# First half batch of attention: output sums ahead of the second weight's joined words on VectorE, and the table for Sin loaded behind the last exponentials

## The chip, the cores and the metric

The kernel runs on one core of a Trainium2 chip (trn2). The metric is the device time of one launch in microseconds (us). The engines are TensorE (PE, with its weight loads as PEld), VectorE (DVE), ScalarE (ACT), GpSimd (POOL) and SyncE (SP, which issues most DMAs).

## The reference, cut to what matters

Three stages follow each other. `sm_attn` is a softmax over the scores times the values; the attention's output is the sum of a pooled and a local one. `w_in` and `w_out` are float64 arrays, the other inputs are float32.

```
# 4 batches, 8 heads, 576 positions, 64 features
out = repeat(sm_attn(q, k, v, each the mean of 4 positions), 4) + sm_attn(q, k, v, |i - j| < 4 only)
x   = out of all heads side by side             # 2304 tokens x 512
h   = x @ w_in                                  # 512 -> 2048
x   = (h * cos(h)) @ w_out                      # 2048 -> 512
e   = argmax(x @ w_gate)                        # one of 8 experts for each token
out = softmax(x @ w_gate)[e] * (relu(x @ w1[e]) @ w2[e])   # 512 -> 1024 -> 512
```

## The kernel before

The middle layer goes over 9 blocks of 256 tokens (i) and 8 pieces of the weights (fp). `hidden(i, fp)` takes 24 matmuls for h, in two float32r parts of x (`xh`, the rounded part, and `xl`, what is left) and two of the weight. Then it forms h·cos(h): ACT rounds h to whole turns (L401), DVE subtracts them (L402), ACT takes Sin (L403) and Square (L404), DVE multiplies (L405), ACT casts to `gh` (L408) and DVE makes the rest `gl` (L409). `project(i, fp)` adds 12 matmuls into the two accumulators of the block (`acc`, L423).

The weights arrive as the 64-bit words of float64. `convert_w(fp, which)` makes two float32r parts of each of the 16 pieces on DVE and POOL, in halves of 512 columns: shift and mask of the high word (L355), the low word's bits or-ed in (L357), the sign joined (L359: the *joined* words), a cast on POOL (L364) and the rest by subtraction on DVE (L366). In the rows of the scheduler's order, `w0_0`, `w1_0`, `w2_0` are pieces 0, 1 and 2 of `w_in` (called in-weights 0, 1, 2 below), and `w0_1`, `w1_1`, `w2_1` those of `w_out` (out-weights 0, 1, 2). Their words stand in `w32_0_1` (in-weight 1), `w32_1_0` (out-weight 0) and so on, with the kind ahead of the piece. The first six are converted in the order of `ORDER`: in 0, in 1, out 0, in 2, out 1, out 2.

The layer can begin when the first 256 tokens of x are there, which is the first half of batch 0 of the attention. So that half batch runs first, its 4 pairs of heads in turn by `together` (a count n goes up with each step of one of them): transposed queries (`tq`), scores (`s`, `sd`), exponentials (`p`, `pd`), their transposes (`pt`, `ptd`, copied by ACT to `pT`, `pdT`), outputs (`o`, L250 and L261), the output sum `xo` on DVE (L263) and then `first_x`, which makes `xh` on ACT (L322) and `xl` on DVE (L323). The first three weights are converted at n = 12, 20 and 28. The second half batch runs beside the first pieces of block 0; `hidden(1, 0)`, the fourth call of `hidden`, needs its x, and the load of the weights from piece 3 on is issued when it is through.

Every engine works off its own queue in order. The order in a queue is fixed when the program is built, by a scheduler; `issue_after(x)` tells it to set an instruction behind x. A wait of one instruction thus holds up all that stands behind it on its engine.

Of the kernel before, what the change touches and what calls it, by code (L numbers as in the profile page):

```python
# [8 lines left out]
F32 = mybir.dt.float32  # L9
# [4 lines left out]
AF = mybir.ActivationFunctionType  # L14
# [5 lines left out]
P = 128  # L20
# [3 lines left out]
NEARLY = 3  # L24
CONV = (12, 20, 28)
POOLED = (12, 12, 13, 14, 15, 16, 17, 18)
# [6 lines left out]
class Kernel:  # L33
# [134 lines left out]

    def queries(self, pool, n, n_, j, qs, raw, hp, kd, kT, vd, vw, sink, behind=None):

# [46 lines left out]
        for t in range(nd):  # L217
            nc.scalar.activation(pd[:m, t, :], ps[:m, t, :], AF.Exp, bias=mxd[:m, t:t + 1], accum_out=smd[:m, t:t + 1])
        self.scaled = nc.gpsimd.tensor_scalar(out=smd[:m, :nd], in0=smd[:m, :nd], scalar1=1e-9, scalar2=4.0,
# [38 lines left out]
        for i in range(nt):  # L258
            for par in range(2):
                r = slice(64 * par, 64 * par + 64)  # L260
                nc.tensor.matmul(ps[r, 64 * i:64 * i + 64], lhsT=vw(i, par), rhs=pT[:, i, r], start=True, stop=True)  # L261
        with self.tc.issue_after(behind()) if behind else nullcontext():
            nc.vector.tensor_tensor(  # L263
                out=x[:, :4 * ng].rearrange("p (g f) -> p g f", f=4),
                in0=ps[:, :4 * ng].rearrange("p (g f) -> p g f", f=4),
                in1=od[:, :ng].unsqueeze(2).to_broadcast([P, ng, 4]), op=ALU.add)
        sink(x)
# [78 lines left out]

    def convert_w(self, fp, which, behind=None):

        nc = self.nc
        t = self.stage.tile([P, 1040], I32, tag="w32", bufs=self.W32, name=f"w32_{which}_{fp}")  # L350
        two = self.words.pop((fp, which)).rearrange("p (n two) -> p n two", two=2)
        halves = [slice(512 * n, 512 * n + 512) for n in range(2)]
        for sl in halves:
            low, high = two[:, sl, 0], two[:, sl, 1]
            nc.vector.tensor_scalar(out=t[:, sl], in0=high, scalar1=3, scalar2=0x3FFFFFFF,  # L355
                                    op0=ALU.logical_shift_left, op1=ALU.bitwise_and)
            nc.vector.scalar_tensor_tensor(out=t[:, sl], in0=low, scalar=29, in1=t[:, sl],  # L357
                                           op0=ALU.logical_shift_right, op1=ALU.bitwise_or)
            self.joined = nc.vector.scalar_tensor_tensor(out=t[:, sl], in0=high, scalar=-0x40000000, in1=t[:, sl],  # L359
                                                         op0=ALU.bitwise_and, op1=ALU.bitwise_or).ins  # L360
        tile = self.w[fp, which] = self.tile_w(fp, which)
# [399 lines left out]
    def run(self):  # L761
# [99 lines left out]
        def first(hp, j):  # L861
            if j == 0:
                q, at = raw["q", 0], hp
            else:
                q, at = ap.tile([P, 4, P], F32, tag="raw", bufs=self.RAWS, name=f"rawq_{hp}"), None
                self.load_rows(q, self.q, 0, hp, 4 * self.HALF[1][0], self.QROWS[1])
            yield from self.queries(pp, 4, f"0_{hp}", j, lanes[hp], q, at, *kv[hp],
                                    lambda kj, par: vd[kj][:, 2 * hp + par, :], lambda i, par: vw[:, i, 2 * hp + par, :],
                                    lambda x: self.first_x(x, hp, j),
                                    (lambda: self.joined) if j == 0 else None)  # L870

        n = 0
        sums = self.summed_values(pp, psh, [raw["v", j] for j in range(2)])
        for _ in self.together([first(hp, 0) for hp in range(4)], 4):
            n += 1
            for _ in range(POOLED.count(n)):
                vd = next(sums)
            if n in CONV:
                with tc.issue_after(self.step):
                    self.convert_w(*early.pop(0), self.scaled)  # L880
        wide.close()
# [206 lines left out]
```

## Time and profile before

| | before |
|---|---|
| median of 3 runs | 876.47 us (875.76 to 877.15) |
| profiled execution | 877.69 us, of which 875.9 us are the span |
| mean granted TensorE clock | 0.979 |
| PE busy | 830.3 us (95%) |
| DVE busy | 537.7 us (61%) |
| ACT busy | 495.4 us (57%) |

The span reaches from the first to the last instruction of the profiled execution. Busy shares are means over the whole span; the first 100 us, where the change lies, are filled otherwise. Times below are us from the span's start.

### The profile page before, as it was taken

To read this page: it belongs to the slowest core of one execution; us is meant where nothing else is said; L and a number is where in the kernel's file an instruction comes from. 1 tells how busy PE (TensorE), PEld (TensorE's weight loads), DVE (VectorE), ACT (ScalarE), POOL (GpSimd) and SP (SyncE) were. 2 spreads that over 40 slices of the span, in tenths; PEclk is the share of its full clock that TensorE was granted. 3 is DMA by queue.
4 is the path that set the end of the run, shared out by engine and by line. 5 is a ranking of instruction groups with operands and counts; after the bars stand their busy time and mean duration, and the time that the engine had idled before them with its cause. 6 is when DMAs were issued, how large, how long until landed. Compare 5 with 4: busy or idle time off the path is not lost.

```text
span 875.9 us, 16801 instructions
## 1 busy us (share of the span) xinstructions
PE 830.3 (95%) x6130; PEld 711.9 (81%) x6130; DVE 537.7 (61%) x1293; ACT 495.4 (57%) x1246; POOL 197.6 (23%) x356
## 2 busy tenths in 40 slices
PE   6889799999999999999999999999899999999995
PEld 4667578778788888788898888898788888888895
DVE  5885799876444485476666657586447654555320
ACT  5466766676766875675644444583366544544321
POOL 5252344442222212313101010100121112012200
PEclk9989899999999999999999999999899999999998
DMA  9931783233252024022010101241748746446110
GB/s 202 290 79 38 295 247 96 71 82 85 59 167 64 14 76 105 13 73 73 15 49 1 49 1 49 73 123 47 192 143 292 243 135 212 148 160 198 58 38 22
DMA packets 112695, 95.87 MB, mean 109 GB/s; under 512 B 65120, under 2 KB 92844, under 8 KB 112604
## 3 DMA queue, kind: packets, MB, share of 16 engines
q1 hardware_dynamic: 108492, 83.96, 32.8%
q0 software_dynamic: 4112, 10.76, 4.1%
q8 instruction: 50, 0.82, 0.4%
q14 instruction: 41, 0.34, 0.1%
HBM read 81.31 MB, written 13.98 MB: 109 GB/s over the span
## 4 chain that ended last, share of the span: by engine, by line
PE 59%; DMA 6%; issue 5%; ACT 5%; DVE 5%; POOL 2%; POOLq 0%; DVEq 0%; ACTq 0%
PE acc L423 16%; PE h L395 15%; PE eacc L671 10%; PE eph L652 9%; DMA lists<-tokens,posi 2%; ACT p L203 1%; DMA raw<-in_moe_w_dram 1%; DMA out_dram<-y,ids 1%; PE o L261 1%; DVE prod L471 1%; PE o L250 1%; PE ext L631 1%; DMA rows<-rows,esrc 1%; PE ptd L238 1%; PE eph_late L689 1%
## 5 line engine op out<-in xcount | busy, mean ns | idle before, releaser
L395 PE MATMUL h<-xh,w 128*128 128x256 f32 x1152 | 230.0, 289 | 0.6 <-ACT xh L322 0.5
L423 PE MATMUL acc<-w,gh 128*128 128x512 f32 x576 | 191.5, 408 | 10.9 <-issue 4.5
L395 PEld LDWEIGHTS h<-xh,w 128*128 128x128 f32 x1152 | 185.8, 192 | 5.5 <-DVE w L366 0.9
L395 PE MATMUL h<-xl,w 128*128 128x256 f32 x576 | 165.4, 287 | 1.4 <-DVE xl L323 1.4
L423 PEld LDWEIGHTS acc<-w,gh 128*128 128x128 f32 x576 | 103.4, 190 | 30.6 <-issue 4.7
L423 PE MATMUL acc<-w,gl 128*128 128x512 f32 x288 | 117.6, 408 | 1.8 <-DVE gl L409 1.8
L652 PE MATMUL eph<-exh,w 128*128 128x256 f32 (+5 forms) x512 | 118.1, 307 | 0.0
L395 PEld LDWEIGHTS h<-xl,w 128*128 128x128 f32 x576 | 110.5, 192 | 4.2 <-DVE xl L323 1.6
L580 DVE TENSOR_TENSOR w<-raw,w 128x512 fp32r<-128x512 f32 x128 | 83.3, 687 | 32.5 <-ACT w L579 32.2
L671 PE MATMUL eacc<-w,hh 128*128 128x512 f32 (+4 forms) x304 | 99.2, 407 | 0.3 <-ACT hh L660 0.3
L652 PEld LDWEIGHTS eph<-exh,w 128*128 128x128 f32 x512 | 87.9, 190 | 3.3
L579 ACT CAST w<-raw 128x512 fp32r<-128x512 f32 x128 | 73.6, 618 | 29.3 <-DMA raw<-in_moe_w_dram 16.3
L401 ACT ACTIVATE u<-h 128x512 int32<-128x512 f32 x72 | 43.2, 600 | 79.7 <-PE h L395 79.6
L652 PE MATMUL eph<-exl,w 128*128 128x256 f32 (+5 forms) x256 | 78.7, 307 | 0.0
L405 DVE SCALAR_TENSOR_TENSOR u<-u,h 128x512 f32<-128x512 f32 x72 | 49.3, 684 | 47.6 <-ACT u L404 47.2
L402 DVE SCALAR_TENSOR_TENSOR u<-h,u 128x512 f32<-128x512 f32 x72 | 49.4, 686 | 38.5 <-ACT u L401 36.3
L471 DVE SCALAR_TENSOR_TENSOR prod<-row,wgb 128x512 f32<-128x512 f32 x96 | 67.1, 699 | 7.4 <-ACT row L465 6.0
L423 PEld LDWEIGHTS acc<-w,gl 128*128 128x128 f32 x288 | 54.5, 189 | 14.4 <-DVE gl L409 2.5
L408 ACT CAST gh<-u 128x512 fp32r<-128x512 f32 x72 | 44.6, 619 | 35.8 <-DVE u L405 21.3
L499 POOL DMA_INDIRECT lists<-tokens,posi x18 | 19.0, 1057 | 198.2 <-DVE posi L496 192.3
L403 ACT ACTIVATE u<-u 128x512 f32<-128x512 f32 x72 | 45.5, 632 | 31.8 <-DVE u L402 30.8
L671 PEld LDWEIGHTS eacc<-w,hh 128*128 128x128 f32 (+4 forms) x304 | 52.1, 182 | 12.0 <-ACT hh L660 0.8
(177 smaller groups left out, 1416.3 us busy)
## 6 DMA issues: line engine op xcount, KB each, us to landing
raw<-in_moe_w_dram SPq DMA_DIRECT2D x64, 512.0 KB
f<-in_moe_w_in_dram SPq DMA_DIRECT2D x8, 1024.0 KB
f<-in_moe_w_out_dram SPq DMA_DIRECT2D x8, 1024.0 KB
rows<-row SPq DMA_DIRECT2D x9, 520.0 KB
xraw<-xT SPq DMA_DIRECT2D x14, 256.0 KB
rawk<-in_k_dram SPq DMA_DIRECT2D x48, 72.0 KB
rawv<-in_v_dram SPq DMA_DIRECT2D x24, 144.0 KB
rawq<-in_q_dram SPq DMA_DIRECT2D x32, 80.0 KB
```

What stands on the lines that cost most here:

```text
L395: nc.tensor.matmul(ph[:, fo, :], lhsT=a[:, kk, f], rhs=b[:, kk, :], start=(n == 0), stop=(n == 3 * self.KD - 1))
L401: nc.scalar.activation(turns, hv, AF.Copy, scale=1.0 / (2 * math.pi))
L402: nc.vector.scalar_tensor_tensor(out=u, in0=hv, scalar=1.0 / (2 * math.pi), in1=turns, op0=ALU.mult, op1=ALU.subtract)
L403: nc.scalar.activation(u, u, AF.Sin, scale=PI)
L405: nc.vector.scalar_tensor_tensor(out=u, in0=u, scalar=1.0, in1=hv, op0=ALU.subtract, op1=ALU.mult, reverse0=True)
L408: nc.scalar.copy(gh, u)
L423: nc.tensor.matmul(self.acc[i][t], lhsT=a[:, fo, t * P:(t + 1) * P], rhs=b[:, fo, :], start=(f == 0 and n == 0), stop=(f == self.NF - 1 an ...
L471: nc.vector.scalar_tensor_tensor(out=prod, in0=row[:, t, :DM], scalar=1.0, in1=self.spread[e // 2][:, e % 2, :], op0=ALU.mult, op1=ALU.mul ...
L579: nc.scalar.copy(hi, raw[:, sl])
L580: nc.vector.tensor_tensor(out=lo, in0=raw[:, sl], in1=hi.bitcast(F32), op=ALU.subtract)
L652: self.lastmm = nc.tensor.matmul(ph, lhsT=a[:, kk, f % 2 * P:(f % 2 + 1) * P], rhs=b[:, kk, :cols], start=(n == 0), stop=(n == 3 * self.KD ...
L671: self.lastmm = nc.tensor.matmul(self.eacc[w][:m], lhsT=a[:, at * P:at * P + m], rhs=b[:, f % 2, :], start=(f == 0 and n == 0), stop=(f == ...
```

## The change

At n = 20 only the shift, mask and or of in-weight 1 (L355 and L357) are issued, by a new function `magnitude`; its sign join, the cast and the subtraction come at n = 28 together with all of out-weight 0. The output sums `xo` of the first half batch no longer are set behind the joined words of in-weight 1. A one-column Sin on a new tile `sine` is issued behind the last exponential of the half batch, and the table for Sin is loaded there. The diff:

```
-CONV = (12, 20, 28)
+CONV, MADE = (12, 28, 28), 20
...
-            nc.scalar.activation(pd[:m, t, :], ps[:m, t, :], AF.Exp, bias=mxd[:m, t:t + 1], accum_out=smd[:m, t:t + 1])
+            self.last = nc.scalar.activation(pd[:m, t, :], ps[:m, t, :], AF.Exp, bias=mxd[:m, t:t + 1], accum_out=smd[:m, t:t + 1]).ins
...
-        with self.tc.issue_after(behind()) if behind else nullcontext():
-            nc.vector.tensor_tensor(
+        nc.vector.tensor_tensor(
...
-    def convert_w(self, fp, which, behind=None):
+    def magnitude(self, fp, which):
...
+        for sl in self.HALVES:
...
-            self.joined = nc.vector.scalar_tensor_tensor(out=t[:, sl], in0=high, scalar=-0x40000000, in1=t[:, sl],
-                                                         op0=ALU.bitwise_and, op1=ALU.bitwise_or).ins
+        return two, t
...
+    def convert_w(self, fp, which, behind=None, made=None):
+
+        nc, halves = self.nc, self.HALVES
+        two, t = made or self.magnitude(fp, which)
+        for sl in halves:
+            nc.vector.scalar_tensor_tensor(out=t[:, sl], in0=two[:, sl, 1], scalar=-0x40000000, in1=t[:, sl],
+                                           op0=ALU.bitwise_and, op1=ALU.bitwise_or)
...
-                                    lambda x: self.first_x(x, hp, j),
-                                    (lambda: self.joined) if j == 0 else None)
+                                    lambda x: self.first_x(x, hp, j))
...
+        sine = pool.tile([P, 1], F32, name="sine")
+        nc.vector.memset(sine, 0.0)
...
-            if n in CONV:
+            for _ in range(CONV.count(n)):
                 with tc.issue_after(self.step):
-                    self.convert_w(*early.pop(0), self.scaled)
+                    self.convert_w(*early.pop(0), self.scaled, made)
+                made = None
+            if n == MADE:
+                with tc.issue_after(self.step):
+                    made = self.magnitude(*early[0])
+                with tc.issue_after(self.last):
+                    nc.scalar.activation(sine, sine, AF.Sin)
```

The line numbers move: what was L355, L357, L359 and L366 is L353, L355, L366 and L373 after the change, L263 is L262, L323 is L322, and L402, L405 and L423 are L409, L412 and L430.

The queues that the scheduler makes differ at three places. On VectorE, at the end of the first half batch, before (behind the last part of in-weight 0):

```order
L355 TENSOR_SCALAR w32_0_1_525<-f64_1_0_269 128x512 x2
L357 SCALAR_TENSOR_TENSOR w32_0_1_525<-f64_1_0_269,w32_0_1_525 128x512 x2
L359 SCALAR_TENSOR_TENSOR w32_0_1_525<-f64_1_0_269,w32_0_1_525 128x512 x2
L263 TENSOR_TENSOR xo_0_0_0_565<-o_0_0_0_537,od_0_0_0_542 128x256
L263 TENSOR_TENSOR xo_0_1_0_577<-o_0_1_0_544,od_0_1_0_549 128x256
L366 TENSOR_TENSOR w1_0_532<-w32_0_1_525,w1_0_532 128x512 x2
L323 TENSOR_TENSOR xl0_280<-xo_0_0_0_565,xh0_279 128x256
L323 TENSOR_TENSOR xl0_280<-xo_0_1_0_577,xh0_279 128x256
L263 TENSOR_TENSOR xo_0_2_0_589<-o_0_2_0_551,od_0_2_0_556 128x256
L263 TENSOR_TENSOR xo_0_3_0_601<-o_0_3_0_558,od_0_3_0_563 128x256
L323 TENSOR_TENSOR xl0_280<-xo_0_2_0_589,xh0_279 128x256
L323 TENSOR_TENSOR xl0_280<-xo_0_3_0_601,xh0_279 128x256
```

The same place after the change:

```order
L262 TENSOR_TENSOR xo_0_0_0_561<-o_0_0_0_533,od_0_0_0_538 128x256
L262 TENSOR_TENSOR xo_0_1_0_573<-o_0_1_0_540,od_0_1_0_545 128x256
L322 TENSOR_TENSOR xl0_280<-xo_0_0_0_561,xh0_279 128x256
L262 TENSOR_TENSOR xo_0_2_0_585<-o_0_2_0_547,od_0_2_0_552 128x256
L353 TENSOR_SCALAR w32_0_1_527<-f64_1_0_269 128x512 x2
L355 SCALAR_TENSOR_TENSOR w32_0_1_527<-f64_1_0_269,w32_0_1_527 128x512 x2
L322 TENSOR_TENSOR xl0_280<-xo_0_1_0_573,xh0_279 128x256
L322 TENSOR_TENSOR xl0_280<-xo_0_2_0_585,xh0_279 128x256
L262 TENSOR_TENSOR xo_0_3_0_597<-o_0_3_0_554,od_0_3_0_559 128x256
L322 TENSOR_TENSOR xl0_280<-xo_0_3_0_597,xh0_279 128x256
L366 SCALAR_TENSOR_TENSOR w32_0_1_527<-f64_1_0_269,w32_0_1_527 128x512 x2
L353 TENSOR_SCALAR w32_1_0_616<-f64_0_1_271 128x512 x2
```

Two output sums, one `xl` and a third sum now stand ahead of the first words of in-weight 1, not only of its joined ones; the join stands behind the last `xl`.

On TensorE, where the transposed queries of the second half batch (`tq`) stand between the matmuls of block 0, before:

```order
L129 MATMUL tq_0_0_1_718<-ident_106,rawq_0_713 128x80 x4
L423 MATMUL acc0_0_1026<-w0_1_620,gl0_0_675 128x512
L423 MATMUL acc0_1_1027<-w0_1_620,gh0_0_674 128x512 x2
L423 MATMUL acc0_1_1027<-w0_1_620,gl0_0_675 128x512
L423 MATMUL acc0_1_1027<-w0_1_620,gh0_0_674 128x512 x2
L129 MATMUL tq_0_1_1_732<-ident_106,rawq_1_727 128x80 x4
L423 MATMUL acc0_1_1027<-w0_1_620,gl0_0_675 128x512
L423 MATMUL acc0_0_1026<-w1_1_986,gh0_1_709 128x512 x2
L423 MATMUL acc0_0_1026<-w1_1_986,gl0_1_710 128x512
L423 MATMUL acc0_0_1026<-w1_1_986,gh0_1_709 128x512 x2
L129 MATMUL tq_0_2_1_746<-ident_106,rawq_2_741 128x80 x4
```

The same place after the change:

```order
L129 MATMUL tq_0_0_1_721<-ident_106,rawq_0_716 128x80 x4
L430 MATMUL acc0_0_1029<-w1_1_989,gh0_1_712 128x512
L430 MATMUL acc0_1_1030<-w1_1_989,gh0_1_712 128x512
L430 MATMUL acc0_0_1029<-w1_1_989,gh0_1_712 128x512
L430 MATMUL acc0_0_1029<-w1_1_989,gl0_1_713 128x512
L430 MATMUL acc0_0_1029<-w1_1_989,gh0_1_712 128x512 x2
L129 MATMUL tq_0_1_1_735<-ident_106,rawq_1_730 128x80 x4
L430 MATMUL acc0_0_1029<-w1_1_989,gl0_1_713 128x512
L430 MATMUL acc0_1_1030<-w1_1_989,gh0_1_712 128x512
L430 MATMUL acc0_1_1030<-w1_1_989,gl0_1_713 128x512
L430 MATMUL acc0_1_1030<-w1_1_989,gh0_1_712 128x512 x2
L430 MATMUL acc0_1_1030<-w1_1_989,gl0_1_713 128x512
```

The second transposed query, `tq_0_1_1`, stood ahead of every matmul with out-weight 1 (`w1_1`) and now stands behind six of them. All 12 matmuls with out-weight 0 now stand ahead of `tq_0_0_1`, against 5 of them before. `tq_0_2_1`, which had 6 matmuls between itself and `tq_0_1_1`, has 6 again, and `tq_0_3_1` follows behind `s_0_0_1`, before with one `acc` more between them.

On ScalarE, behind the last exponential of the first half batch, before:

```order
L218 ACTIVATE pd_0_3_0_435,smd_0_3_0_434<-sd_0_3_0_436,mxd_0_3_0_433 128x144
L231 COPY pT_0_0_0_458<-pt_0_0_0_459 70x512
L231 COPY pT_0_1_0_466<-pt_0_1_0_467 70x512
L165 COPY vd0_0_474<-vds0_443 72x512
L231 COPY pT_0_2_0_476<-pt_0_2_0_477 70x512
L231 COPY pT_0_3_0_485<-pt_0_3_0_486 70x512
```

The same place after the change:

```order
L218 ACTIVATE pd_0_3_0_437,smd_0_3_0_436<-sd_0_3_0_438,mxd_0_3_0_435 128x144
L231 COPY pT_0_0_0_460<-pt_0_0_0_461 70x512
L894 ACT_TABLE_LOAD
L894 ACTIVATE sine_283<-sine_283 128x1
L231 COPY pT_0_1_0_468<-pt_0_1_0_469 70x512
L165 COPY vd0_0_476<-vds0_445 72x512
L231 COPY pT_0_2_0_478<-pt_0_2_0_479 70x512
L231 COPY pT_0_3_0_487<-pt_0_3_0_488 70x512
```

The table load of L403, which stood between the two L401 of block 0, is gone from there; the order on ScalarE up to the next load (that of L203 for the second half batch) otherwise holds the same instructions.

## Rows read from the trace of the kernel before

**Rows 1.** The page: busy us (share of the span) and instructions of each engine.

```profile
PE 830.3 (95%) x6130; PEld 711.9 (81%) x6130; DVE 537.7 (61%) x1293; ACT 495.4 (57%) x1246; POOL 197.6 (23%) x356
```

**Rows 2.** Windows: us; busy (count) of PE, PEld, DVE, ACT, POOL; clock; DMA share, GB/s.

```profile
41.60:46.05 4.45, 0.00 (x0) 0.03 (x1) 4.45 (x10) 2.87 (x6) 0.07 (x1) 0.83 0.66 149
46.05:48.20 2.15, 2.15 (x5) 1.19 (x5) 2.15 (x4) 0.62 (x1) 1.56 (x2) 0.50 0.71 161
...
61.00:75.00 14.00, 11.09 (x64) 8.25 (x61) 9.98 (x27) 10.65 (x58) 10.23 (x20) 0.88 0.18 42
```

**Rows 3.** Timeline of TensorE: start, us, instruction, [idle before <-what ended it].

```profile
29.91 2.04 PE L261 MATMUL o<-pT,vw 70*64 70x64 f32 x62
...
34.27 0.54 PE L395 MATMUL h<-xl,w 128*128 128x256 f32 x1 [1.37 <-DVE xl L323]
...
46.05 0.77 PE L423 MATMUL acc<-w,gh 128*128 128x512 f32 x1 [4.50 <-issue]
...
54.52 0.44 PE L129 MATMUL tq<-ident,rawq 80*128 80x80 f32 x4
54.75 0.48 PE L423 MATMUL acc<-w,gl 128*128 128x512 f32 x1
...
56.23 0.44 PE L129 MATMUL tq<-ident,rawq 80*128 80x80 f32 x4
...
57.85 0.44 PE L129 MATMUL tq<-ident,rawq 80*128 80x80 f32 x4
```

**Rows 4.** Timeline of VectorE, the same columns.

```profile
28.34 0.76 DVE L355 TENSOR_SCALAR w<-f 128x512 int32<-128x512 int32 x2 [1.95 <-DMA f<-in_moe_w_in_dram]
...
31.43 0.75 DVE L263 TENSOR_TENSOR xo<-o,od 128x256 f32<-128x256 f32 x2
32.22 1.67 DVE L366 TENSOR_TENSOR w<-w,w 128x512 fp32r<-128x512 f32 x2
...
39.75 0.69 DVE L402 SCALAR_TENSOR_TENSOR u<-h,u 128x512 f32<-128x512 f32 x1 [0.55 <-ACT u L401]
40.36 1.28 DVE L366 TENSOR_TENSOR w<-w,w 128x512 fp32r<-128x512 f32 x2
41.56 0.76 DVE L355 TENSOR_SCALAR w<-f 128x512 int32<-128x512 int32 x2
...
43.43 0.69 DVE L402 SCALAR_TENSOR_TENSOR u<-h,u 128x512 f32<-128x512 f32 x1
44.03 0.68 DVE L405 SCALAR_TENSOR_TENSOR u<-u,h 128x512 f32<-128x512 f32 x1
...
53.17 0.69 DVE L402 SCALAR_TENSOR_TENSOR u<-h,u 128x512 f32<-128x512 f32 x1 [0.73 <-ACT u L401]
...
54.17 1.34 DVE L366 TENSOR_TENSOR w<-w,w 128x512 fp32r<-128x512 f32 x2
```

**Rows 5.** Timeline of ScalarE, the same columns.

```profile
22.03 0.58 ACT L231 COPY pT<-pt 70x512 f32<-70x512 f32 x1 [0.72 <-PE pt L230]
22.89 0.58 ACT L165 COPY vd<-vds 72x512 f32<-72x512 f32 x1 [0.28 <-PE vds L162]
...
31.88 0.73 ACT L322 CAST xh<-xo 128x256 fp32r<-128x256 f32 x2 [1.53 <-DVE xo L263]
...
39.74 1.28 ACT L403 ACT_TABLE_LOAD   x1
41.03 0.63 ACT L403 ACTIVATE u<-u 128x512 f32<-128x512 f32 x1
...
45.35 0.60 ACT L408 CAST gh<-u 128x512 fp32r<-128x512 f32 x1
...
60.08 0.32 ACT L203 ACTIVATE p<-s,mx 128x70 f32<-128x70 f32 x1
...
69.90 0.38 ACT L218 ACTIVATE pd<-sd,mxd 80x144 f32<-80x144 f32 x1 [2.32 <-DVE mxd L216]
```

**Rows 6.** TensorE's waits from 28 to 100 us.

```profile
PE acc L423 <- POOL w L364: 2.8, 1, 2.8
```

More of the change, by code (lines that the diff above doesn't have):

```diff
@@ L167, in summed_values, with queries @@
                 yield vd
-    def queries(self, pool, n, n_, j, qs, raw, hp, kd, kT, vd, vw, sink, behind=None):
+    def queries(self, pool, n, n_, j, qs, raw, hp, kd, kT, vd, vw, sink):
         nc, S = self.nc, self.S
@@ L261, in queries @@
                 nc.tensor.matmul(ps[r, 64 * i:64 * i + 64], lhsT=vw(i, par), rhs=pT[:, i, r], start=True, stop=True)
-        with self.tc.issue_after(behind()) if behind else nullcontext():
-            nc.vector.tensor_tensor(
-                out=x[:, :4 * ng].rearrange("p (g f) -> p g f", f=4),
-                in0=ps[:, :4 * ng].rearrange("p (g f) -> p g f", f=4),
-                in1=od[:, :ng].unsqueeze(2).to_broadcast([P, ng, 4]), op=ALU.add)
+        nc.vector.tensor_tensor(
+            out=x[:, :4 * ng].rearrange("p (g f) -> p g f", f=4),
+            in0=ps[:, :4 * ng].rearrange("p (g f) -> p g f", f=4),
+            in1=od[:, :ng].unsqueeze(2).to_broadcast([P, ng, 4]), op=ALU.add)
         sink(x)
@@ L351, in convert_w @@
         two = self.words.pop((fp, which)).rearrange("p (n two) -> p n two", two=2)
-        halves = [slice(512 * n, 512 * n + 512) for n in range(2)]
-        for sl in halves:
+        for sl in self.HALVES:
             low, high = two[:, sl, 0], two[:, sl, 1]
@@ L358, in convert_w @@
                                            op0=ALU.logical_shift_right, op1=ALU.bitwise_or)
-            self.joined = nc.vector.scalar_tensor_tensor(out=t[:, sl], in0=high, scalar=-0x40000000, in1=t[:, sl],
-                                                         op0=ALU.bitwise_and, op1=ALU.bitwise_or).ins
+        return two, t
+    HALVES = [slice(512 * n, 512 * n + 512) for n in range(2)]
+    def convert_w(self, fp, which, behind=None, made=None):
[4 more added lines that the diff above has]
+                                           op0=ALU.bitwise_and, op1=ALU.bitwise_or)
         tile = self.w[fp, which] = self.tile_w(fp, which)
@@ L868, in first @@
                                     lambda kj, par: vd[kj][:, 2 * hp + par, :], lambda i, par: vw[:, i, 2 * hp + par, :],
-                                    lambda x: self.first_x(x, hp, j),
-                                    (lambda: self.joined) if j == 0 else None)
-        n = 0
+                                    lambda x: self.first_x(x, hp, j))
+        n, made = 0, None
+        sine = pool.tile([P, 1], F32, name="sine")
+        nc.vector.memset(sine, 0.0)
         sums = self.summed_values(pp, psh, [raw["v", j] for j in range(2)])
```

## The prediction

> **What bounds the kernel now.** I read the page first: PE is busy 95% of the span and DVE 61% [rows 1], so over the whole run whatever makes TensorE wait is paid, and DVE looks free. The second view, busy time in windows, corrects this for the stretch of the change. From 41.60 to 46.05 PE does nothing at all while DVE is busy 4.45 of 4.45 us, and from 46.05 to 48.20 DVE is again full, with PE at a granted clock of 0.50, half speed [rows 2]. The reader is to see that DVE, converting weights, is the limit here, and that a mean of 61% hides it.
>
> The timelines then say what is done in which order. On TensorE, the outputs of the first half batch end near 31.9, the first matmul of h on `xl` waits until 34.27, the first `acc` starts at 46.05 after 4.50 us of idling ("issue" names no one, but the `gh` that it needs is cast on ACT from 45.35, right ahead), and transposed queries of the second half batch come at 54.52, 56.23 and 57.85 [rows 3, 5]. On VectorE, the words of in-weight 1 begin at 28.34, when their DMA lands, and take until 31.43, which is 3.09 us; from there to the end of out-weight 1 (54.17 + 1.34 = 55.51) the rows that wait do so for 0.55 and 0.73 us only [rows 4].
>
> **What the change does, part by part.**
>
> *The sums go ahead of the words.* DVE's queue is in order, so the first `xo` now holds the words of in-weight 1 behind it. That sum needs all 16 local matmuls of `o_0`. The 62 of row 29.91 spread over 2.04 us [rows 3]; two had started earlier, so `o_0` has its last after 14 of them, at 29.91 + 14/62 x 1.8 + 0.2, about 30.5 (an estimate from that row). Today DVE fills the time before with words from 28.34 [rows 4]. From now on it stands idle till 30.5: **2.2 us of DVE lost**, just where DVE becomes the limit.
>
> Does x come sooner in return? Two sums and `xl_0` do (31.4; today the first `xl` stands behind an L366 that ends at 32.22 + 1.67 = 33.89 [rows 4]), but `xl_1` stands behind four word instructions. From 30.5, four instructions of x and two pairs of words (3.09 us for three pairs, about 1.9 for these) end near 33.9, and `xl_1` near 34.4. h waited for `xl` until 34.27 [rows 3]. So h starts its run where it did: nothing won, nothing lost. What is lost besides is a stall at the last `xl`: it follows its own `xo` directly, and the cast between them on ACT starts 0.45 after the sum started (31.43 to 31.88 [rows 4, 5]), so DVE waits about 0.5.
>
> *The chain of the first `gh`.* Two things get better here. The table load of 1.28 us leaves the chain: Sin starts at 41.03, and could have started when the first L402 ended, 39.75 + 0.69 = 40.44; the load costs 0.59 [rows 4, 5]. And in the new order the first words of in-weight 2 (41.56 to 43.43, 1.87 us [rows 4]) no longer stand ahead of the first L405. Against it: DVE reaches the first L402 at 39.75 - 0.55 + 2.2 + 0.5 = 41.9. Behind it follow L366 of out-weight 0 (1.28 to 1.67), the second L402 and the first L405 (0.6 each), so L405 starts near 44.8 where it was 44.03, and the cast of `gh`, which stands behind Sin and Square of the second block half on ACT, near 46.2 instead of 45.35 [rows 4, 5]. **First acc: +0.8** (46.85), in spite of both gains.
>
> On the load there is a rule to weigh. The row shows the next ACTIVATE 0.01 us after the load's end (39.74 + 1.28 = 41.02, start 41.03 [rows 5]). The Trainium skill ("ScalarE: Activation LUTs", section "What ACT_TABLE_LOAD costs") has a drain of about 1.38 us on top of a load of about 1.28. The trace agrees on the load and shows no drain ahead of the next instruction. By the rule the moved load would hold ACT 1.4 us longer in its new place, where little covers it, and the sum below would be 883.2 in place of 881.8.
>
> In its new place the load stands ahead of `pT_1`. There ACT idles 0.72 and 0.28 now [rows 5]; load and Sin of one column take about 1.5, so `pT` and `vd` come up to 0.8 late and later idle time takes that in. I cost it at 0; without that cover it would be 0.8, with o and everything behind it.
>
> *Out-weight 1, the next hand-over.* All 12 matmuls of out-weight 0, then h of the third piece, then out-weight 1. Its last L366 ended at 55.51. Now: +2.2 for the late start, +0.5 for the last `xl`, -0.55 and -0.73 for the two waits that a late DVE no longer has, -1.0 for L402 of the third piece and one `qd` (53.17 to 54.17) that now stand behind, +0.7 for a pair of words of out-weight 2 that now stand ahead (0.76 by row 41.56), +0.8 for two pairs of L366 that now run right beside POOL's cast (1.67 in place of 1.28, as at 32.22 and 40.36 [rows 4]). **Sum +1.9: 57.4.** Bounds +1.1 (no slowing beside POOL) and +2.3.
>
> *The transposed queries.* `tq_1` had 11 `acc` of block 0 ahead of it, now 18. `acc` take 1.48 for six (54.75 to 56.23 [rows 3]), 0.25 each. By PE's work alone: 54.52 + 0.8 + 7 x 0.25 = 57.1. But its six with out-weight 1 need the weight that is there at 57.4, and one or two follow that: 57.8, **+3.3**. From `tq_1` to `tq_3` it took 57.85 - 54.52 = 3.33 with seven `acc` in between; now six, so 3.0, or up to 1.5 more if they fall in a stretch at half clock, as the one behind the idle of 46.05 did [rows 2, 3]. I take 3.4: `tq_3` at 61.2, **+3.4** (+2.5 to +4.5).
>
> *The rest of the second half batch* hangs on it: the exponentials start 2.23 behind `tq_3` (60.08 [rows 5]), and ACT, DVE and POOL hand on to each other up to the x of block 1, which the fourth `hidden` needs. `sd_1` now also stands behind the first `acc` of out-weight 2, which waits 2.8 for POOL's cast today [rows 6]; I add **0.6** (0 to 2).
>
> *Batch 1.* The weights from piece 3 on are loaded when that half batch ends, so they come late by the same amount. In DVE's new queue three more word instructions, 0.6 to 0.7 each, stand ahead of the pooled keys of the second head pair, for which PE's scores wait. Between 0 and 3; I take **1.3**, two of the three.
>
> PE's own work is the same, so the idle time adds: 3.4 + 0.6 + 1.3 = 5.3. Profiled execution 877.69 + 5.3 = 883.0; it lies 1.2 above the median of the runs shown (876.47), so the median to expect is **881.8 us**. What a measurement of this kernel can tell from no change is about 0.2%, 1.75 us.
>
> **The rivals.**
>
> 1. *The late shift grows.* Batch 1 takes its upper bound (3.0), the stretch at half clock falls on `tq`, and `sd_1` waits: 4.5 + 1 + 3 = 8.5, 885.0. For it: every queue behind 60 us is fixed beforehand, and late weights meet instructions that stand behind them. Against: slack of 2.9 us of PE in 61 to 75 [rows 2].
> 2. *Slack takes it in: no change.* ACT idles 2.32 ahead of `pd` for `mxd` [rows 5], which stands behind the L366 of out-weight 2 on DVE. If the late scores only fill that wait, 3.4 - 2.3 = 1.1 stays, and nothing behind: 877.6, within 0.2%. Against: in the new queue that L366 still stands ahead of `mxd`, so the wait moves along.
> 3. *Faster: the chain of `gh` wins.* 0.59 for the load and 1.87 for the words come off the 4.50 us that PE waits: 876.47 - 2.46 = 874.0. It decides if the lost 2.2 us of DVE are no loss, that is if DVE is through to the first L402 by 39.8 in the new order too. For that the words of in-weight 1 would have to land at 30.5 or later, or `o_0` be ready by 28.5. Against: they landed at 28.34 and DVE has waits of 0.55 and 0.73 only [rows 4].
> 4. *The load has no cover* on ACT: +0.8 on top, 882.6, inside my range.
>
> **Numbers.** My forecast (879.3 to 884.0, with rival 4) 0.54; rival 1 (above 884) 0.21; rival 2 0.12; rival 3 0.13. The likeliest one's own range is 879.3 to 884.0 (the bounds +2.5 and +4.5 of `tq_3` with 0.3 to 3 behind them). For 8 in 10 the range must take in rival 2 and most of rival 1, but neither rival 3 nor the upper 0.06 of rival 1: 876.8 to 885.8. Slower by over 0.2%: 0.54 + 0.21 = 0.75; within: 0.12; faster: 0.13.
>
> **What would show it.** In the profile after: DVE idle from about 26.4 (28.34 - 1.95 [rows 4]) to 30.5, ended by PE's `o` (the first step; if it ends by 28.5, rival 3 lives); first L402 at 41.9; first `acc` at 46.9; L366 of out-weight 1 ending at 57.4; `tq` near 55, 57.8, 60 and 61.2; the first exponential of the second half batch at 63.4. If `tq_3` comes by 59, the count of matmuls ahead of it was no loss. If it comes at 61 but the fourth `hidden` starts less than 2 later than at present, rival 2 was right; if PE waits for keys grow between 100 and 170, rival 1. The prediction is wrong as a whole if PE's idle ahead of the first `acc` gets shorter than 4.5.

## The result and the profile after

| | before | after |
|---|---|---|
| median of 4 runs | 876.34 us (875.76 to 877.15) | 884.86 us (883.45 to 888.53) |
| profiled execution | 877.69 us, span 875.9 us | 888.53 us, span 886.8 us |

The ratio is 1.0103 with a 95% interval of 1.0071 to 1.0135: the change makes the kernel 8.5 us slower. The profiled execution is the longest of the four; 883.45 is the shortest. So a shift read from the trace after stands up to 5 us above that of a shorter run.

The page of after first, its busy row as in [rows 1]:

```profile
PE 835.8 (94%) x6130; PEld 716.1 (81%) x6130; DVE 536.8 (61%) x1294; ACT 498.4 (56%) x1249; POOL 196.8 (22%) x356
```

Span less busy time is the time in which TensorE stood: 886.8 - 835.8 = 51.0, before 875.9 - 830.3 = 45.6. So of the 10.9 us by which the span is longer, 5.4 are idle time of PE, and the other 5.5 are PE being longer at the same 6130 matmuls. This second part is the clock. The next views show where both arise. VectorE's timeline of after, the stretch of [rows 4]:

```profile
30.06 0.89 DVE L262 TENSOR_TENSOR xo<-o,od 128x256 f32<-128x256 f32 x2 [2.88 <-PE o L261]
...
31.63 0.75 DVE L353 TENSOR_SCALAR w<-f 128x512 int32<-128x512 int32 x2
...
35.06 0.42 DVE L322 TENSOR_TENSOR xl<-xo,xh 128x256 fp32r<-128x256 f32 x1 [0.47 <-ACT xh L321]
...
37.69 1.70 DVE L373 TENSOR_TENSOR w<-w,w 128x512 fp32r<-128x512 f32 x2
...
41.72 0.68 DVE L409 SCALAR_TENSOR_TENSOR u<-h,u 128x512 f32<-128x512 f32 x1
...
44.70 0.67 DVE L412 SCALAR_TENSOR_TENSOR u<-u,h 128x512 f32<-128x512 f32 x1
...
56.63 1.67 DVE L373 TENSOR_TENSOR w<-w,w 128x512 fp32r<-128x512 f32 x2 [0.51 <-POOL w L371]
```

VectorE waits 2.88 us for `o`; the words of in-weight 1 begin at 31.63 and not at 28.34. TensorE of after, as in [rows 3]:

```profile
46.71 1.19 PE L430 MATMUL acc<-w,gh 128*128 128x512 f32 x2 [5.01 <-issue]
...
55.18 0.44 PE L129 MATMUL tq<-ident,rawq 80*128 80x80 f32 x4
...
57.75 0.65 PE L430 MATMUL acc<-w,gh 128*128 128x512 f32 x1 [0.37 <-DVE w L373]
...
59.47 0.73 PE L129 MATMUL tq<-ident,rawq 80*128 80x80 f32 x4
...
62.07 0.44 PE L129 MATMUL tq<-ident,rawq 80*128 80x80 f32 x4
...
63.35 0.50 PE L129 MATMUL tq<-ident,rawq 80*128 80x80 f32 x4
...
70.65 0.50 PE L430 MATMUL acc<-w,gh 128*128 128x512 f32 x1 [2.57 <-POOL w L371]
```

In TensorE's list of waits after, over the whole span, stands one for keys in batch 1 that the list of before does not hold (us in total, times, longest):

```profile
PE tk L129 <- DVE kd L140: 2.2, 2, 1.6
```

`tq_0` to `tq_3` are the transposed queries of the four pairs of heads. The first `acc` is 0.7 later, `tq_1` 4.9 and `tq_3` 5.5 (57.85 to 63.35). ScalarE of after, at the load's new place:

```profile
21.62 1.28 ACT L894 ACT_TABLE_LOAD   x1
22.92 0.20 ACT L894 ACTIVATE sine<-sine 128x1 f32<-128x1 f32 x1
23.03 0.56 ACT L231 COPY pT<-pt 70x512 f32<-70x512 f32 x1
```

The load is followed by its Sin after 0.02 us. The Trainium skill ("ScalarE: Activation LUTs", section "What ACT_TABLE_LOAD costs") has a drain of about 1.38 us beside the load; this row, like the one of before [rows 5], shows the 1.28 and no drain.

Last, four windows of after (columns as in [rows 2]):

```profile
57.90:61.30 3.40, 3.40 (x11) 2.68 (x12) 2.59 (x6) 1.02 (x3) 0.52 (x3) 0.51 0.05 13
71.60:78.40 6.80, 5.96 (x19) 4.89 (x18) 2.61 (x7) 2.48 (x14) 4.09 (x10) 0.50 0.11 25
...
143.30:150.10 6.80, 6.80 (x46) 5.46 (x45) 3.35 (x7) 3.11 (x6) 1.22 (x3) 0.50 0.15 40
242.30:249.10 6.80, 6.80 (x25) 5.49 (x25) 2.69 (x17) 1.51 (x3) 0.00 (x0) 0.50 0.14 52
```

And three windows of before:

```profile
100.00:150.00 50.00, 48.17 (x444) 40.55 (x443) 47.43 (x96) 33.49 (x105) 22.91 (x44) 1.00 0.63 191
150.00:200.00 50.00, 47.56 (x435) 39.39 (x434) 40.78 (x86) 35.95 (x111) 23.70 (x45) 1.00 0.27 68
200.00:250.00 50.00, 48.24 (x432) 40.90 (x430) 25.73 (x73) 32.18 (x82) 13.31 (x26) 1.00 0.34 89
```

Between 100 and 250 us before has full clock throughout. After has 0.50 in 143.30 to 150.10 and in 242.30 to 249.10 with PE busy without a gap: work at 1.2 in place of 2.4 GHz. An estimate from the 6.80 us of each: half the time would have done at full clock, so each cost some 3.4 us.

To follow the loss through the program, the same matmul is looked up in both traces, and the difference of its starts taken: +0.7 at the first `acc`, +7.0 at the first matmul of the fourth hidden (81.3 before), +11.7 at the one that stood at 155 us before, +10.4 at 216, +14 from 235 to 340, about +11 at the end.

Two stretches of the same work, up to the first matmul of the fourth hidden and from there to the one that stood at 230 us, in before:

```profile
0.00:81.32 81.32, 64.97 (x619) 49.60 (x620) 58.48 (x149) 45.93 (x171) 35.05 (x88) 0.92 0.62 157
81.32:230.00 148.68, 138.69 (x1250) 115.62 (x1248) 116.60 (x245) 102.29 (x293) 58.15 (x110) 0.98 0.47 138
```

The same in after:

```profile
0.00:88.29 88.29, 68.93 (x619) 52.48 (x620) 59.64 (x150) 45.61 (x172) 33.98 (x88) 0.88 0.57 145
88.29:241.50 153.21, 140.35 (x1251) 117.17 (x1249) 114.99 (x245) 105.59 (x296) 58.94 (x110) 0.96 0.45 134
```

Of the +7.0 at the fourth hidden, 3.0 is idle time of PE (16.35 to 19.36), and 4.0 is the same 619 matmuls at a lower clock (0.92 to 0.88). In the second stretch the idle time grows by 2.9 (9.99 to 12.86).

### The profile page after: what moved, and what is told of

It reads as the page before. It is cut to its first block, busy times and chain, and to the rows that moved or that the text cites. A ratio compares the mean times of both kernels' runs of the same rounds, so it can differ in the third digit from the quotient of the medians.

```text
span 886.8 us, 16807 instructions
## 1 busy us (share of the span) xinstructions
PE 835.8 (94%) x6130; PEld 716.1 (81%) x6130; DVE 536.8 (61%) x1294; ACT 498.4 (56%) x1249; POOL 196.8 (22%) x356
## 4 chain that ended last, share of the span: by engine, by line
PE 58%; issue 10%; DVE 9%; DMA 8%; ACT 8%; POOL 5%; SPq 1%; POOLq 0%; DVEq 0%; ACTq 0%
PE acc L430 18%; PE h L402 15%; PE eacc L678 10%; PE eph L659 8%; ACT p L203 2%; DMA raw<-in_moe_w_dram 2%; DVE w L373 2%; DMA lists<-tokens,posi 2%; PE o L261 1%; DMA rawv<-in_v_dram 1%; DMA rows<-rows,esrc 1%; PE o L250 1%; ACT L203 1%; POOL w L371 1%; DMA out_dram<-y,ids 1%
## 5 line engine op out<-in xcount | busy, mean ns | idle before, releaser
L402 PE MATMUL h<-xh,w 128*128 128x256 f32 x1152 | 228.5, 288 | 1.2 <-DVE w L373 0.8
L430 PE MATMUL acc<-w,gh 128*128 128x512 f32 x576 | 197.4, 417 | 13.2 <-issue 5.0
L402 PEld LDWEIGHTS h<-xh,w 128*128 128x128 f32 x1152 | 184.6, 190 | 5.7 <-DVE w L373 1.3
L402 PE MATMUL h<-xl,w 128*128 128x256 f32 x576 | 164.3, 285 | 1.9 <-DVE xl L322 1.9
L430 PEld LDWEIGHTS acc<-w,gh 128*128 128x128 f32 x576 | 106.6, 195 | 34.0 <-issue 5.2
L430 PE MATMUL acc<-w,gl 128*128 128x512 f32 x288 | 119.1, 414 | 1.5 <-DVE gl L416 1.5
L402 PEld LDWEIGHTS h<-xl,w 128*128 128x128 f32 x576 | 109.9, 191 | 4.4 <-DVE xl L322 2.3
L412 DVE SCALAR_TENSOR_TENSOR u<-u,h 128x512 f32<-128x512 f32 x72 | 49.2, 684 | 49.9 <-ACT u L411 49.6
L409 DVE SCALAR_TENSOR_TENSOR u<-h,u 128x512 f32<-128x512 f32 x72 | 49.3, 685 | 37.3 <-ACT u L408 36.6
L430 PEld LDWEIGHTS acc<-w,gl 128*128 128x128 f32 x288 | 55.8, 194 | 14.6 <-DVE gl L416 2.5
L410 ACT ACTIVATE u<-u 128x512 f32<-128x512 f32 x72 | 45.5, 632 | 28.9 <-DVE u L409 28.5
```

The source lines that it names most:

```text
L402: nc.tensor.matmul(ph[:, fo, :], lhsT=a[:, kk, f], rhs=b[:, kk, :], start=(n == 0), stop=(n == 3 * self.KD - 1))
L409: nc.vector.scalar_tensor_tensor(out=u, in0=hv, scalar=1.0 / (2 * math.pi), in1=turns, op0=ALU.mult, op1=ALU.subtract)
L410: nc.scalar.activation(u, u, AF.Sin, scale=PI)
L412: nc.vector.scalar_tensor_tensor(out=u, in0=u, scalar=1.0, in1=hv, op0=ALU.subtract, op1=ALU.mult, reverse0=True)
L430: nc.tensor.matmul(self.acc[i][t], lhsT=a[:, fo, t * P:(t + 1) * P], rhs=b[:, fo, :], start=(f == 0 and n == 0), stop=(f == self.NF - 1 an ...
```

## The experiments

All ratios are to the kernel before on the same chip, with the 95% interval. "Shift" is the lookup just described, in the profiled executions, against before. Each trace is of one execution: in before and experiments 6 and 9, whose queues lead VectorE and ScalarE in the same order up to it, the first `acc` comes at 46.05, 47.02 and 47.10. So a difference of under 1 us between two traces says little.

**1. The load alone (e1_load_only).** Before, with the one-column Sin behind the last exponential, and nothing else.

```
+            if n == 20:
+                with tc.issue_after(self.last):
+                    nc.scalar.activation(sine, sine, AF.Sin)
```

> Before, with nothing but the one-column Sin behind the last exponential; sums and words stay as they were. Theory A (the loss comes from VectorE's late start and the queries behind out-weight 1): VectorE's words begin at 28.3 as before, the load is off the chain of the first gh, first acc at 43 to 46, no loss: 873 to 877 us. Rival B (the load in its new place costs, by a drain or by pushing the copies of pT): o late by 1 us or more, 878 us or more. Rival C (any new order of the queues behind 60 us costs, whatever the first 60 us do): 880 or more.

Measured: 898.68 us, ratio 1.021 (1.0136 to 1.0284), worse than the whole change. VectorE starts as before and the first `acc` comes at 44.21, 1.8 us earlier: up to there the move of the load wins. But a load in another place also makes the scheduler lay out other queues. In them the transposes `pt` follow the scores closely, with no matmuls of block 0 between, and PE has to wait for each. TensorE's timeline:

```profile
67.86 0.69 PE L215 MATMUL sd<-kd,qdbd 128*80 128x144 f32 x4 [0.81 <-POOL w L364]
69.66 0.60 PE L230 MATMUL pt<-ident,p 128*70 128x128 f32 x4 [0.54 <-POOL p L206]
71.67 0.60 PE L230 MATMUL pt<-ident,p 128*70 128x128 f32 x4 [1.41 <-ACT pd L218]
```

The window behind these waits:

```profile
73.00:90.00 17.00, 16.68 (x156) 14.13 (x157) 6.38 (x21) 8.09 (x26) 0.56 (x3) 0.50 0.08 17
```

17 us at half clock follow, with PE busy 16.68 of them. The first `pt` comes 2.8 us earlier than before, since those `acc` no longer stand ahead of it; but `tq_3` comes 1.6 later (59.42), and so does the first exponential on ScalarE (61.65 for 60.08). The shift at the fourth hidden is +5.6. On the page of this kernel PE is busy 846.9 of 897.7 us: 5.2 us more idle time than before, as in after, but 16.6 more busy time.

**2. The sums alone, all queues scheduled anew (e2_order_only).** After, without the Sin and its tile.

```
-                with tc.issue_after(self.last):
-                    nc.scalar.activation(sine, sine, AF.Sin)
```

> After, without the one-column Sin: sums ahead of the words, load back on the chain of the first gh. Theory A: VectorE idle until 30 as in after, first acc at 47 to 48.5, tq_3 at 62 to 65, 883 to 888 us. Rival B: without the moved load the loss is gone, 875 to 878.

Measured: 892.94 us, 1.0124 (1.0055 to 1.0192), beside 1.0103 with the load moved. The load is back in the chain of the first `gh` (43.36 on ScalarE) and the first `acc` comes at 48.24, 1.5 later than in after. At the fourth hidden the shift is +7.4, in after +7.0. So the load's place is worth 1.5 us at the first `acc` and nothing at the hand-over that counts.

**3. The sums behind the or-ed words (e3_words_first).** After, with `xo` set behind the second word step of in-weight 1, so that VectorE does not stand idle.

```
+        with self.tc.issue_after(behind()) if behind else nullcontext():
...
+            self.ored = nc.vector.scalar_tensor_tensor(out=t[:, sl], in0=low, scalar=29, in1=t[:, sl],
...
+                                    (lambda: self.ored) if j == 0 else None)
```

> After, with the output sums set behind shift, mask and or of in-weight 1 (not behind its sign join): the words begin at 28.3 again, all else of the change is kept. Theory A: 2.2 us of VectorE are back, first acc at 44.5 to 45.5, second query behind one matmul of out-weight 1 instead of six, 874 to 879 us. Rival C (order behind 60 us, stretches at half clock): stays at 881 or more.

Measured: 894.01 us, 1.0121 (1.0065 to 1.0176). The words begin at 29.00, as their DMA lands, and the first `acc` comes at 46.05, where before had it (44.5 to 45.5 was expected). `tq_3` comes at 59.66 and the first exponential at 61.88: 3.7 us earlier than in after, and still 1.8 later than before. So VectorE's order was mended for the most part. The gain is not kept: half clock from 68.8 to 92.7, shift +6.4 at the fourth hidden and +18 at 235 us, where PE waits 3.59 us for `p` (a `pt` at 242.99). The expected time was missed, in the way of experiment 1: with the sums behind the words again, and queues laid out anew, the time does not come back.

**4. The transposed queries ahead (e4_queries_ahead).** After, with out-weight 1's matmuls of block 0 behind the last `tq`.

```
+                    with self.tc.issue_after(self.last_tq) if (i, fp) == (0, 1) else nullcontext():
```

> After, with the matmuls of out-weight 1 of block 0 set behind the last of the four transposed queries; VectorE still starts late. Theory A as in the prediction, whose larger part is the queries' place: first acc at 46.7 as in after, but all four queries by 57, exponentials from 58 to 60, fourth hidden at 82 or earlier, 874 to 879 us. Rival D (VectorE's lateness holds the half batch up anyway, through the words of out-weight 2 and mxd): fourth hidden at 85 or later, 881 or more.

Measured: 891.72 us, 1.0107 (1.0076 to 1.0138). Three of the four queries come by 56.74, the fourth only at 61.51, and the first exponential at 64.83: the signs of rival D. The fourth hidden starts 3.2 us earlier than in after (shift +3.8). By one trace of each, the queries' place costs that much in after's queues; part of it is clock, which was 0.50 from 71.60 to 78.40 in after and is 1.00 here. By 155 us the shift is +6.2, and at 237.06 the wait for `p` stands again (3.07) and it is +12.5. The time is no better.

Experiments 1 to 4 move the time by the queues of batch 1 as much as by what they were to test. The next ones keep all queues behind 75 us as they are in before.

**5. The sums alone, the other queues kept (e5_sums_free).** Before, with only the order of `xo` set free.

```
-                                    lambda x: self.first_x(x, hp, j),
-                                    (lambda: self.joined) if j == 0 else None)
+                                    lambda x: self.first_x(x, hp, j))
```

> Before, with only the rule taken away that sets the output sums behind the joined words of in-weight 1: no split, no moved load. On VectorE the sums stand first as in after, on TensorE the second query stands behind matmuls of out-weight 1 as in after; from 75 us on all queues are those of before. Theory A (VectorE's late start and the queries' place): fourth hidden 3 to 7 us later than before and the loss stays to the end, ratio to before 1.004 to 1.009. Rival C (the new order from 75 us on costs): ratio within 0.998 to 1.002.

Measured: 888.32 us (883.00 to 893.74), 1.0106 (1.0065 to 1.0147); the profiled execution is the shortest. TensorE's timeline:

```profile
49.66 1.19 PE L423 MATMUL acc<-w,gh 128*128 128x512 f32 x2 [5.09 <-issue]
...
63.46 0.44 PE L129 MATMUL tq<-ident,rawq 80*128 80x80 f32 x4
```

First `acc` +3.6, `tq_3` +5.6, fourth hidden +4.7, then +3.8 through batch 1 and about +6 at the end. With the queues of batch 1 untouched, the sums ahead of the words cost as much as the whole change, within the intervals. They do so earlier: the first `acc` is 3.6 late here and 0.7 in after, where the split of the words and the moved load win some of it back (1.5 of it the load, experiment 2). And the trace is of the shortest of the six runs: its span is 5.4 us longer than that of before, the whole change's 10.9.

**6. The idle of TensorE filled in before (e6_before_filled).** 14 useless matmuls of 128x512 into `acc0_0` stand in the 4.50 us of [rows 3]; the first real matmul overwrites them.

```
+                for n in range(fill[0]):
+                    nc.tensor.matmul(self.acc[i][0], lhsT=self.x[i][0][:, n % 4, :P], rhs=self.x[i][0][:, 0:2, :].rearrange("p a b -> p (a b)"),
+                                     start=True, stop=True)
```

> Before, with 14 matmuls of 512 columns that compute nothing needed, put into TensorE's wait ahead of the first acc; VectorE's, ScalarE's and GpSimd's queues are those of before. Theory K (a wait of TensorE costs twice, once by itself and once by the stretch at half clock behind it): the stretch from 44.6 to 51.4 goes or gets shorter, 1 to 3.5 us won at the first transposed query, ratio 0.996 to 1.000. Rival (the half clock has nothing to do with the wait): stretch stays, ratio 1.000 or, where the added matmuls delay the first acc, up to 1.002.

Measured: 879.39 us, 1.000 (0.9971 to 1.0028). One window in before:

```profile
44.60:51.40 6.80, 5.35 (x20) 4.41 (x21) 6.80 (x13) 1.94 (x4) 1.63 (x2) 0.50 0.38 86
```

The same window in this kernel:

```profile
44.60:51.40 6.80, 5.47 (x31) 4.13 (x30) 6.80 (x12) 2.39 (x4) 1.63 (x2) 1.00 0.43 97
```

With PE kept at work the clock stays at 1.00. In this execution the first `acc` comes 1.0 later than in before, behind 1.33 us of waiting for `gh`, and `tq_1` only 0.15 later (54.67): full clock won about 0.8 us back. At the fourth hidden the shift is -0.2. VectorE is busy 6.80 of 6.80 in both windows, and TensorE now waits for weights that it did not wait for before (0.62 us for out-weight 1). So half clock in this stretch costs next to nothing at the fourth hidden; the times, with 2.5 us to either side, can't tell it from nothing.

**7. The same in after (e7_after_filled).** The same lines.

> After, with the same 14 matmuls in the wait ahead of the first acc. Theory K: no half clock between 44 and 51, queries 2 to 3.5 us earlier, ratio to before 1.003 to 1.008 against 1.010 of after. Rival: as after, 1.009 to 1.012.

Measured: 892.21 us, 1.014 (1.0105 to 1.0175). The filling did not do here what it was to do. The half clock moved instead of going away:

```profile
48.90:52.40 3.50, 3.50 (x10) 2.25 (x9) 3.50 (x7) 0.62 (x1) 0.94 (x2) 0.51 0.00 0
```

It lasts 3.5 us where after had 6.8 (44.30 to 51.10), and nothing came back: the first `acc` at 47.81, `tq_1` at 60.39, fourth hidden +8.1. That this stretch is no large part of after's loss is made likely by this, and not shown.

**8. The waits of experiment 1 filled (e8_load_only_filled).** Useless matmuls with the identity among the scores and transposes of the second half batch.

```
+        for _ in range(6 if n_ in ("0_1_1", "0_2_1", "0_3_1") else 0):
+            nc.tensor.matmul(ps[:, 0, :P], lhsT=self.ident, rhs=self.ident, start=True, stop=True)
```

> The kernel with the moved load alone (1.021), with small matmuls of the identity that compute nothing needed in the waits of the second half batch (18 ahead of sd, 24 ahead of pt, 0.1 us each); the queues stay as they were. Theory K: the stretch at half clock from 73 to 90 goes, which cost some 8 us there, fourth hidden 5 to 8 us earlier, ratio 1.010 to 1.015. Rival (the half clock is a consequence of something else than TensorE's waits, or the waits alone are the loss): stretch stays, ratio 1.020 to 1.025.

Measured: 901.63 us, 1.0214 (1.0162 to 1.0267). The stretch at 73 to 90 is gone, and the time is that of experiment 1 all the same. The profiled execution was already 10.5 us late at the first `o`, at half clock from 19.5 to 50.3, so the trace can't say what the stretch was worth: inconclusive.

**9. The transposed queries ahead in before (e9_before_queries_ahead).** The edit of experiment 4 in before; 20 matmuls change places.

> Before, with nothing changed but TensorE's queue between 55 and 63 us: the third and fourth transposed queries stand ahead of all matmuls of out-weight 1 (20 matmuls change places; the queues of VectorE, ScalarE and GpSimd are those of before). Theory A, by which the place of the queries sets the half batch: tq_3 at 56.3 instead of 57.85, exponentials 1.5 us earlier, fourth hidden up to 1.5 us earlier, ratio 0.997 to 1.000. Rival D (the words of out-weight 2 and the waits for mxd set the half batch): fourth hidden where it was, ratio 0.999 to 1.002.

Measured: 880.10 us, 1.0001 (0.9971 to 1.0032); `tq_3` at 57.51 (56.3 was expected; the first `acc` is 1.0 late in this execution) and the fourth hidden where it was. With VectorE in time, the place of the queries is worth nothing that these times show.

**10. Experiment 5 with the queries ahead (e10_sums_free_queries_ahead).** Both edits together, later queues kept.

> The kernel with the free sums alone (1.0106), with all four transposed queries ahead of the matmuls of out-weight 1; VectorE still starts its words late, and from 75 us on all queues are those of before. If the queries' place is the larger part (A): tq_3 at 60 or earlier instead of 63.5, fourth hidden 3 us earlier than without, ratio 1.001 to 1.006. If VectorE's lateness alone is (D): fourth hidden at most 1 us earlier, ratio 1.008 to 1.012.

Measured: 886.81 us, 1.0042 (1.0009 to 1.0074). TensorE's timeline:

```profile
58.75 0.99 PE L129 MATMUL tq<-ident,rawq 80*128 80x80 f32 x12
...
61.24 0.50 PE L129 MATMUL tq<-ident,rawq 80*128 80x80 f32 x4
...
63.45 0.31 PE L195 MATMUL s<-mask,ident 128*128 128x350 bf16 x1 [0.52 <-DVE qd L183]
```

`tq_3` comes 2.2 us earlier than in experiment 5, but the scores then wait for `qd`, which stands on VectorE, and the fourth hidden wins 0.5 (+4.2 for +4.7). By the trace most of the loss stays without the matmuls ahead of `tq`; by the times (1.0042 and 1.0106, intervals that overlap) the size of their part isn't settled.

**11. The load in a third place (e11_load_late).** Experiment 1 with the Sin behind the last `xh` cast; apart from ScalarE the queues are those of experiment 1.

```
+            cast = nc.scalar.copy(hi, x[:, done:done + n])
+            if j == 0 and hp == 3:
+                with self.tc.issue_after(cast.ins):
+                    nc.scalar.activation(self.sine, self.sine, AF.Sin)
```

> The kernel with the moved load alone (1.021), with the load set behind the last cast of xh, 14 us later, where ScalarE idles; every queue but ScalarE's four places is that of the moved load alone. Rival B (the load ahead of the copies of pT costs): ratio falls to 1.005 or below. Theory C for that kernel (the new queues cost, not the load): ratio stays at 1.017 to 1.025.

Measured: 901.30 us, 1.0239 (1.0188 to 1.0289); fourth hidden +5.8, in experiment 1 +5.6. The load at 35.67 in place of 21.77 changes nothing, so its place behind the exponentials is not what experiment 1 pays for. What the two share, and before does not, is the order of the other queues.

**12. VectorE relieved (e12_rests_on_gpsimd).** Before, with the subtractions of in-weight 1 and out-weight 0 on GpSimd; later queues kept.

```
-            nc.vector.tensor_tensor(out=tile[:, 1024 + sl.start:1024 + sl.stop], in0=t[:, sl].bitcast(F32),
+            (nc.gpsimd if (fp, which) in ((1, 0), (0, 1)) else nc.vector).tensor_tensor(out=tile[:, 1024 + sl.start:1024 + sl.stop], in0=t[:, sl].bitcast(F32),
```

> The kernel before, with the four subtractions of in-weight 1 and out-weight 0 (L366) on GpSimd in place of VectorE; every other instruction stays, and from about 75 us on all queues are those of before. Theory A (VectorE's work ahead of the first output sums of the middle layer is the bound of this stretch): VectorE is relieved of two pairs, 1.67 and 1.28 us, so the wait of TensorE for the first gh gets shorter by 1 to 2.5 us (first acc at 43.5 to 45.0 in place of 46.05), tq_3 and the fourth hidden come 1 to 2.5 us earlier, and the ratio to before is 0.997 to 0.999. Theory E (GpSimd is too slow at subtractions, so its result is late): the third piece of h or the first acc waits for GpSimd, the first acc comes at 46 or later, the fourth hidden not earlier, ratio 1.000 or above.

Measured: 886.30 us, 1.0085 (1.0054 to 1.0115). By its signs the theory that GpSimd is late held, but not by its reason. GpSimd's timeline:

```profile
41.67 2.73 POOL L366 TENSOR_TENSOR w<-w,w 128x512 fp32r<-128x512 f32 x2
```

VectorE's, beside the subtractions of in-weight 1 (32.98 to 35.88 on GpSimd) and at the same time as those above:

```profile
32.70 3.46 DVE L323 TENSOR_TENSOR xl<-xo,xh 128x256 fp32r<-128x256 f32 x3
...
42.08 2.60 DVE L355 TENSOR_SCALAR w<-f 128x512 int32<-128x512 int32 x2
```

The pair takes 2.73 us on GpSimd, up to 1.70 on VectorE. And while it runs, a pair of words on VectorE takes 2.60, in before 0.76 [rows 4]. It ends 0.3 us behind the subtractions (44.68 and 44.40). The first pair does the same to three `xl`, which take 3.46 us, where two took 0.75 in before, and end at 36.16. So the relief is lost, in-weight 2 comes late, and the third h waits 4.45 us for it: named is GpSimd's cast, but GpSimd stood for 2.76 us ahead of that cast and waited for VectorE's words. The scheduler also set this h ahead of the first `acc`, which comes at 52.98, so the kernel is no clean test of a relieved VectorE. The Trainium skill ("SBUF — State Buffer", section "Who interferes with whom") has a pair of ports that both engines share, and where instructions of both need it, the one that issues first holds it to its end and the other is blocked; the rows agree. No version was found that beats the kernel before.

## Why the prediction came out right, and where it was off

**Sign and first mechanism: right.** 881.8 was forecast; 884.86 was measured, in the range and near rival 1 (885.0), 0.9 above the likeliest case's own range. That the sums ahead of the words are a loss is shown by experiment 5 (the sums alone lose as much). That VectorE is the bound of the stretch is read from its full windows, and experiment 6 fits it (a faster TensorE there gains nothing at the fourth hidden). It is not the whole loss: experiment 3 mends VectorE's order and is no faster.

**The front of the chain: right.** VectorE stands until 30.06 (forecast 30.5), 1.7 us behind the 28.34 at which the words started before (2.2); 0.47 at the last `xl` (0.5); first L402 at 41.72 (41.9); first L405 at 44.70 (44.8); first `acc` +0.7 (+0.8). Experiments 6 and 9 have before's order on VectorE and ScalarE up to the first `acc` (47.02 and 47.10), experiments 4 and 7 after's (47.73 and 47.81): the mean difference is 0.7 again. h starts at 33.97 (34.27), so nothing was won there, as forecast.

**Out-weight 1: somewhat short.** Its last L366 ends at 56.63 + 1.67 = 58.30 and not at 57.4. A wait of 0.51 for GpSimd's cast was not counted, nor that the pair of shifts at 50.26 beside a cast takes 1.17 and not 0.75; the pairs beside that cast took 1.67 to 1.70 as assumed.

**The transposed queries: the first mis-sized term.** `tq_3` +5.5 where +3.4 was forecast, over the upper bound of 4.5. Of the 2.1 more, 0.9 is the weight; the rest fell to matmuls at clock 0.51 from 57.90 to 61.30, which the prediction had only as a bound and in rival 1. Its reading that the matmuls ahead of `tq` carry the loss was too strong: in after's queues they cost some 3 us at the fourth hidden (4), in the queues of before nothing (9) or 0.5 (10).

**The rest of the half batch: somewhat short.** +4.0 was forecast at the fourth hidden, +7.0 measured. Of the 3.0 more, 2.1 had come by `tq_3`; this term itself is 1.5 where 0.6 (0 to 2) was taken. The wait for out-weight 2's cast is no longer than before (2.57, 2.8 in [rows 6]), but 0.84 for its L373 comes behind it, and then 6.8 us at half clock (71.60 to 78.40). Before has a shorter one there:

```profile
68.50:71.90 3.40, 3.40 (x12) 2.38 (x11) 1.86 (x5) 1.13 (x6) 2.53 (x6) 0.50 0.00 0
```

**Batch 1: the second, and for another reason.** 1.3 was forecast; +4.7 had come by 155 us and 3.5 more at 235. The waits for keys that rival 1 asked for are there (1.6 + 0.6 us), and two stretches at half clock of some 3.4 each. The prediction took the term as lateness and three instructions ahead of the keys. The traces put most of it down to the new order as a whole: the queues differ at more than the three places named ahead of the prediction, TensorE's up to 216 us and VectorE's up to 220. With before's order behind 75 us (experiments 5, 10 and 12) the fourth hidden is late by 4.2 to 6.1, and the shift grows by only 0.3 to 0.8 more up to 300 us. With a new order (after and experiments 1 to 4, 7, 8 and 11) it grows by 5.2 to 13.8. From 230 to 270 us the granted clock is 0.87 to 0.91 in all eight traces with a new order, and 1.00 in all six with before's.

**The sum.** "PE's own work is the same, so the idle time adds" is the sentence that failed. The idle time did add 5.4 us, where 5.3 were forecast. That is in part luck: 3.0 had come by the fourth hidden (4.0 forecast), 2.9 came behind it up to 241.50 (1.3 forecast), and the rest idles 0.5 less. And the same work took 5.5 us longer in the profiled execution, at a mean clock of 0.971 in place of 0.979; the sum has no term for that. The shortest run of after had 0.979 too and was 883.45: 5.8 above the profiled run of before, which is about the idle time alone (no trace of that run was kept).

**The load.** Costed at 0 in its new place, and it is: `pT_1` comes 1.0 later (23.03 for 22.03), and the copies of `pdT` start at 25.00 for 25.60, so later idle time took it in as forecast (experiment 11 agrees). Rivals 2, 3 and 4 are out: the late scores were not taken in, the 5.01 us ahead of the first `acc` did not shrink, and what came late on ScalarE was made up for.

**Open.** Why experiment 5, with before's order behind 75 us, has the same ratio as the whole change, where the traces say that this order saves some 6 us in batch 1: its kept trace is of its shortest run (883.00), and none of a run like its longest (893.74, clock 0.965). What in the new order leads to the two stretches at half clock in batch 1: each lies behind a wait of TensorE (1.19 us for `pd` at 141.42, 1.32 for `p` at 240.53), and no run took these waits away alone. And what a stretch at half clock in the second half batch costs (experiment 8).

## What to carry to other kernels

Where an engine with a mean of 61% is full in one stretch, its in-order queue there is what counts: an instruction that waits for another engine must not stand ahead of work that is ready, even if its result is wanted sooner. Idle time of TensorE may be paid twice, as the wait and as half clock on the work behind it (experiment 6: 0.50 became 1.00 when the wait was filled; there it was worth next to nothing, since VectorE was the limit); look for both, and add up idle and busy time of the page apart. And where a scheduler lays out the queues, an edit that wins at one hand-over (the load: 1.8 us at the first `acc`) can lose 2% elsewhere, so compare the queues far behind the edit, and test with the later ones kept.

## What was not expected of the hardware

How much a pair of subtractions on GpSimd takes from VectorE: 1.84 us of the 2.73 (2.60 less 0.76, experiment 12), more than the 1.28 to 1.70 that the pair takes on VectorE itself, so that moving it off gains nothing. The casts that stand on GpSimd anyway cost VectorE's subtractions about 0.4 us for a pair (1.67 to 1.70, and 1.28 without). Filling 4.5 us of TensorE's idle with matmuls of no use kept the granted clock at 1.00 where it had been 0.50 (experiment 6), and the run was no shorter.
